# One reordering and one reshaped load in a load-bound decode kernel: denominators and last transposition moved, part of w2 in eight-row transfers

## Chip, cores, metric

One core of one Trainium2 chip. The metric is device time in microseconds (us) of one execution. The kernel before has a median of 191.76 us over six runs (190.99 to 192.43). The profiled run of the kernel before took 190.90 us, less than any of the six. A number read from a profile is therefore compared with profiled runs, a median with medians.

## The reference, cut to what matters

```python
xn = layernorm(x)                         # x: 2 x 1 x 448
q  = xn @ wq                              # 16 heads of 256
k, v = the last 4096 rows of the caches   # 8 kv heads, 2 batches: 16 pairs of 2 MB each
p  = softmax(q @ k.T / 16)
A  = (p @ v) @ wo
h  = xn @ w1 + b1
B  = (h * tanh(softplus(h))) @ w2         # w1: 448 x 1792, w2: 1792 x 448
return x + A + B
```

It is 77.7 MB of caches and weights read once, against little arithmetic. The kernel must keep the loads going.

## The kernel before: the parts concerned

`P` is 128. `i` counts the 16 pairs (kv head, batch). All large loads are issued by SP (SyncE), in program order. PE is TensorE, ACT ScalarE, DVE in the profiles VectorE. `kt` is the transposed k, `den` the sum in a softmax denominator, `psA` the accumulated output. A load counts as landed at the last count of its completion semaphore, the counter that others wait on.

```python
x_bf ... nc.scalar.dma_start(...)         # x, then b1, issued by ACT
for lo, hi in ((0, SC), (SC, NS)):        # wq in two parts, by SP
    nc.sync.dma_start(out=w, in_=wq_in[:, lo:hi, :])
# ... cut ...
def load_dense():
    dense["w1"] = v_tile(NS * HF)...
    nc.sync.dma_start(out=dense["w1"], in_=B_w1...)
    dense["w2"] = v_tile(NX * NF * D).rearrange("p (x c d) -> p x c d", x=NX, c=NF)
    nc.sync.dma_start(                    # one transfer, 128 rows
        out=dense["w2"], in_=B_w2.rearrange("(x q c) d -> q x c d", x=NX, q=P))
# ... cut ...
def turn_p(s):                            # VectorE: transpose exp(scores); then, for the second half:
    nc.vector.transpose(out=pT[:], in_=p_t.pop(s)[:])
    # ... cut ...  sums from the row sums (two VectorE instructions)
    nc.tensor.matmul(den[:], lhsT=ones_f[:], rhs=sums[:], start=True, stop=True)
    nc.vector.reciprocal(out=state["rec", i][:], in_=den[:])
# ... cut ...
load_k(0)
load_dense()
load_k(1)
project(); build_q(0); build_q(1); turn(0)
NFIX = 5                                  # so many last pairs use 64 narrow matmuls (values_fixed)
for i in range(NK + KA):                  # NK = 16, KA = 2
    if i + 2 < NK:
        load_k(i + 2)
    if i < NK:
        load_v(i, ...); # load_wo every second pair
        for half in range(NH):
            s = i * NH + half
            if s + 1 < NSTEP: turn(s + 1) # VectorE: transpose half of k
            scores(s)                     # PE, then ACT exp
            if s >= 1: turn_p(s - 1)
            if half == 0 and i > KA: close(i - KA - 1)   # finish a head, mix in wo
    if i == NK:
        turn_p(NSTEP - 1)
        close(i - KA - 1)
    # ... cut: dense_in at i == 0, dense_out at i == 1 ...
    if i >= KA: values(i - KA) or values_fixed(i - KA)
    if i >= NK: close(i - KA)
```

In this document k1 is the second k to be loaded (`load_k(1)`), head 13 is pair 13, and so on; "small" transfers are the eight new ones.

The softmax here doesn't subtract the row's maximum and nothing guards it: scores larger than these inputs give would overflow.

Of the kernel before, what the change touches and what calls it, by code (L numbers as in the profile page):

```python
# [12 lines left out]
FP32 = mybir.dt.float32  # L13
# [21 lines left out]
def kernel(  # L35
# [13 lines left out]
    nc = tc.nc  # L49
    P = 128  # L50
    Q = 32
    NQ = P // Q

    Bsz, Sq, D = A_x.shape
    _, Hkv, Sk, Dh = A_k_cache.shape
    HqDh = A_wq.shape[1]
    Hq = HqDh // Dh
    rep = Hq // Hkv
# [6 lines left out]
    NX = 2  # L65
    NS = D * NX // P
    HW = HqDh // NX
    HF = F // NX
    HH = Hq // NX
    NF = HF // P  # L70
    ND = Dh // P
    NB = Dh // (2 * Q)
    NE = 2
# [15 lines left out]
    small = ctx.enter_context(tc.tile_pool(name="small", bufs=3))  # L89
# [9 lines left out]
    b1_sb = consts.tile([1, F], BF16)  # L99
# [3 lines left out]
    def v_tile(n):  # L103
        t = v_pool.tile([P, T * Dh], BF16, tag="v", name="v")
        return t[:, 0:n]
# [6 lines left out]
    for lo, hi in ((0, SC), (SC, NS)):  # L112
# [18 lines left out]
        out=rstd[:], in_=mv[:, 1:2], func=ACT.Sqrt, bias=eps_t[:], scale=1.0  # L131
# [80 lines left out]
    def add(lhsT, w, start=False, stop=False):  # L212
        for n in range(NO):
            nc.tensor.matmul(  # L214
                part(n),
                lhsT=lhsT,
                rhs=w[:, n * DO : (n + 1) * DO],
                start=start,
                stop=stop,
                tile_position=(0, n * Q),  # L220
                skip_group_check=True,
            )
# [47 lines left out]
    act_bf = consts.tile([P, NF, NX, Bsz], BF16)  # L270
    dense = {}

    def load_dense():
        dense["w1"] = v_tile(NS * HF).rearrange("p (s n) -> p s n", s=NS)
        nc.sync.dma_start(  # L275
            out=dense["w1"],
            in_=B_w1.rearrange("r (x n) -> (r x) n", x=NX).rearrange("(p s) n -> p s n", s=NS),
        )
        dense["w2"] = v_tile(NX * NF * D).rearrange("p (x c d) -> p x c d", x=NX, c=NF)
        nc.sync.dma_start(  # L280
            out=dense["w2"], in_=B_w2.rearrange("(x q c) d -> q x c d", x=NX, q=P)
        )

    def dense_in():
        w1_v = dense.pop("w1").rearrange("p s (q c) -> p s c q", c=NF)
        b1_v = b1_sb[:].rearrange("o (x q c) -> o x c q", x=NX, c=NF)
        hT_ps = ps_m.tile([P, NF, NX, Bsz], FP32, tag="m", name="hT_ps")
        for c in range(NF):
            for s in range(NS):
                nc.tensor.matmul(  # L290
                    hT_ps[:, c, :, :].rearrange("p x b -> p (x b)"),
                    lhsT=w1_v[:, s, c, :],
                    rhs=xs[:, s, :, :].rearrange("p x b -> p (x b)"),
                    start=(s == 0),
                    stop=False,
                    skip_group_check=True,
                )
            for x in range(NX):
                nc.tensor.matmul(
                    hT_ps[:, c, x, :],  # L300
                    lhsT=b1_v[:, x, c, :],
                    rhs=ones[:, :],
                    start=False,
                    stop=True,
                    skip_group_check=True,
                )
        shape = [P, NF, NX, Bsz]
        h_sb = consts.tile(shape, FP32, name="h_sb")
        nc.vector.tensor_copy(out=h_sb[:], in_=hT_ps[:])
        u_sb = consts.tile(shape, FP32, name="u_sb")  # L310
        nc.scalar.activation(out=u_sb[:], in_=h_sb[:], func=ACT.Exp)
        t_sb = consts.tile(shape, FP32, name="t_sb")
        nc.vector.scalar_tensor_tensor(
            out=t_sb[:], in0=u_sb[:], scalar=2.0, in1=u_sb[:], op0=ALU.add, op1=ALU.mult
        )
        den = consts.tile(shape, FP32, name="den_sb")
        nc.vector.tensor_scalar(
            out=den[:], in0=t_sb[:], scalar1=2.0, scalar2=None, op0=ALU.add
        )
        nc.vector.reciprocal(out=den[:], in_=den[:])  # L320
        nc.vector.tensor_tensor(out=t_sb[:], in0=t_sb[:], in1=den[:], op=ALU.mult)
        nc.vector.tensor_tensor(out=act_bf[:], in0=h_sb[:], in1=t_sb[:], op=ALU.mult)

    def dense_out():
        w2_sb = dense.pop("w2")
        for x in range(NX):
            for c in range(NF):
                add(act_bf[:, c, x, :], w2_sb[:, x, c, :])


    NSTEP = len(heads) * NH
# [63 lines left out]
    def turn_p(s):  # L395
        pT = p_pool.tile([P, TH * Q], BF16, tag="pT", name="pT", bufs=7)
        nc.vector.transpose(out=pT[:], in_=p_t.pop(s)[:])  # L397
        pT_t[s] = pT
        i, half = divmod(s, NH)
        if half != NH - 1:  # L400
            return
        rs = state.pop(("rs", i))
        sums = small.tile([P, rep], FP32, tag="sums", name="sums")
        nc.vector.tensor_scalar(  # L404
            out=sums[:], in0=hsel, scalar1=rs[:, 0:1], scalar2=None, op0=ALU.mult
        )
        nc.vector.scalar_tensor_tensor(  # L407
            out=sums[:], in0=hsel, scalar=rs[:, 1:2], in1=sums[:], op0=ALU.mult, op1=ALU.add
        )
        den = ps_m.tile([P, rep], FP32, tag="m", name="den")  # L410
        nc.tensor.matmul(den[:], lhsT=ones_f[:], rhs=sums[:], start=True, stop=True)  # L411
        state["rec", i] = small.tile([P, rep], FP32, tag="rec", name="rec", bufs=4)
        nc.vector.reciprocal(out=state["rec", i][:], in_=den[:])  # L413

    NP = 2
    NR = NP * rep
# [1 line left out]
    def values(i):  # L418

        po = ps_o.tile([NR, NP * Dh], FP32, tag="o", name="o")  # L420
        v = v_t.pop(i)
        for u in range(T // NP):
            half, uh = divmod(u, TH // NP)
            nc.tensor.matmul(  # L424
                po[:],
                lhsT=pT_t[i * NH + half][:, uh * NP * Q : (uh + 1) * NP * Q : HS],
                rhs=v[:, u * NP : (u + 1) * NP, :].rearrange("p t d -> p (t d)"),
                start=(u == 0),
                stop=(u == T // NP - 1),
            )  # L430
        o_sb = small.tile([NR, NP * Dh], FP32, tag="o_sb", name="o_sb", bufs=1)
        nc.scalar.copy(out=o_sb[:], in_=po[:])  # L432
        state["o", i] = o_sb

    def scale_o(i, o):
        kvh, b = heads[i]
        if b == 0:
            state["oT"] = small.tile([P, ND, rep, Bsz], BF16, tag="oT", name="oT")
        nc.vector.tensor_tensor(  # L439
            out=state["oT"][:, :, :, b],  # L440
            in0=o,
            in1=state.pop(("rec", i))[:].unsqueeze(1).to_broadcast([P, ND, rep]),
            op=ALU.mult,
        )

# [14 lines left out]

    def values_fixed(i):

        pq = ps_q.tile([P, NP * ND * NR], FP32, tag="q", name="q")
        po = pq[:, 0 : ND * rep].rearrange("p (c h) -> p c h", c=ND)
        vv = v_t.pop(i).rearrange("p t (m c) -> p t c m", c=ND)
        for t in range(T):
            half, th = divmod(t, TH)
            pTv = pT_t[i * NH + half][:].rearrange("p (t c) -> p t c", t=TH)
            for c in range(ND):
                nc.tensor.matmul(  # L470
                    po[:, c, :],
                    lhsT=vv[:, t, c, :],
                    rhs=pTv[:, th, 0:Q:HS],
                    start=(t == 0 and c == 0),
                    stop=(t == T - 1),
                    skip_group_check=True,
                )
        scale_o(i, po)
# [19 lines left out]
    build_q(0)  # L498
    build_q(1)
    turn(0)  # L500
    NFIX = 5

    def close(i):
        if i < NK - NFIX:
# [5 lines left out]
    for i in range(NK + KA):  # L510
# [3 lines that stand above are left out]
            load_v(i, (0, T) if i < NK - 1 else (0, T // 2, 3 * T // 4, T))  # L514
            kvh, b = heads[i]
            if b == Bsz - 1:
                load_wo(kvh, parts=1 if i < NK - 1 else 2)
            for half in range(NH):
                s = i * NH + half
                if s + 1 < NSTEP:  # L520
                    turn(s + 1)
                scores(s)
                if s >= 1:
                    turn_p(s - 1)
                if half == 0 and i > KA:
                    close(i - KA - 1)
            if i + 2 < NK:
                build_q(i + 2)
        if i == NK:
            turn_p(NSTEP - 1)  # L530
            close(i - KA - 1)
        if i == 0:
            dense_in()
        if i == 1:
            dense_out()
        if i >= KA:
            if i - KA < NK - NFIX:
                values(i - KA)
            else:
                values_fixed(i - KA)  # L540
        if i >= NK:
            close(i - KA)
# [37 lines left out]
```

## Time and profile before

| | before |
|---|---|
| time, median of 6 | 191.76 us |
| span of the profiled run (190.90 us) | 189.1 us |
| bytes read | 77.67 MB |
| DMA queue of SP, share of 16 engines' span | 97.1% |
| PE busy | 77% |
| VectorE waits for k | 37.2 us |
| last load (second half of the last wo) lands | 183.55 to 185.33 us, by engine |

### The profile page before, as it was taken

The numbers are of one execution on the slowest core, as the hardware profiler recorded it, in microseconds if no ns is written. First come the engines' busy times: TensorE is split into PE (matmuls) and PEld (weight loads), VectorE is DVE, ScalarE is ACT, GpSimd is POOL, SyncE is SP. The second block draws the span as 40 slices with busy tenths as digits, with TensorE's granted clock in tenths as the row PEclk, the third lists the DMA queues.
The fourth block names the chain that finished last, engine by engine and source line by source line (L and its number), as shares of the span: only waits on it lengthen the run. The fifth ranks groups of instructions, "written<-read, shape, count | busy, mean of one in ns | idle before, by whom it ended". The sixth has DMA issues, their size and how long they took to land.

```text
span 189.1 us, 3026 instructions
## 1 busy us (share of the span) xinstructions
PE 145.6 (77%) x1202; PEld 71.1 (38%) x1202; DVE 113.5 (60%) x193; ACT 32.0 (17%) x81; POOL 27.6 (15%) x139
## 2 busy tenths in 40 slices
PE   0142992696997799949996899779994996598973
PEld 0142381142442435323533235233532344252572
DVE  5705506988839392857658582939376764839221
ACT  6000110112122013111212022201221121110201
POOL 8004430031130030203030023003020300000000
PEclk9999996699999789997999699978999799955855
DMA  6999999999999999999999999999999999999990
GB/s 215 419 444 414 431 438 426 437 428 430 418 423 433 437 421 431 426 437 407 448 430 428 433 419 433 430 426 418 442 437 426 414 435 433 425 430 423 415 381 27
DMA packets 7816, 77.86 MB, mean 412 GB/s; under 512 B 757, under 2 KB 2809, under 8 KB 3322
## 3 DMA queue, kind: packets, MB, share of 16 engines
q1 hardware_dynamic: 7796, 77.66, 97.1%
q8 instruction: 9, 0.15, 0.3%
q14 instruction: 5, 0.04, 0.1%
q10 hardware_dynamic: 6, 0.01, 0.0%
HBM read 77.67 MB, written 0.00 MB: 411 GB/s over the span
## 4 chain that ended last, share of the span: by engine, by line
DMA 70%; DVE 21%; PE 6%; SPq 1%; issue 1%; ACT 0%; ACTq 0%
DMA k<-in_A_k_cache_dram 70%; DVE kt L364 14%; DVE pT L397 4%; PE q L470 3%; PE sc L376 1%; PE den L411 1%; DVE sums L407 1%; PE psA L214 1%; DVE sums L404 0%; SPq L114 0%; DVE oT L439 0%; SPq L275 0%; SPq L280 0%; SPq L338 0%; DVE rec L413 0%
## 5 line engine op out<-in xcount | busy, mean ns | idle before, releaser
L364 DVE STREAM_TRANSPOSE kt<-k 128x2048 f32<-128x2048 f32 x32 | 73.3, 2292 | 37.2 <-DMA k<-in_A_k_cache_dram 37.2
L376 PE MATMUL sc<-kt,qdiag 128*128 128x512 bf16 x256 | 75.2, 445 | 9.9 <-DVE kt L364 9.7
L376 PEld LDWEIGHTS <-qdiag 128*128 128x128 bf16 x256 | 25.6, 109 | 48.9 <-issue 28.0
L264 POOL COPY qdiag<-qrep 32x8 bf16<-32x8 bf16 x128 | 23.3, 215 | 122.9 <-PE sc L376 108.3
L424 PE MATMUL o<-v,pT 128*4 128x512 bf16 x176 | 39.8, 379 | 0.0
L386 ACT ACTIVATE p<-sc 128x512 bf16<-128x512 f32 x32 | 19.1, 597 | 105.1 <-PE sc L376 103.1
L424 PEld LDWEIGHTS <-pT 128*4 128x4 bf16 x176 | 14.4, 87 | 25.7 <-issue 5.8
L397 DVE STREAM_TRANSPOSE pT<-p 128x512 bf16<-128x512 bf16 x32 | 21.5, 672 | 0.0
L411 PE MATMUL den<-sums,ones_f 128*128 128x2 f32 x32 | 5.9, 253 | 15.5 <-DVE sums L407 15.4
L411 PEld LDWEIGHTS den<-sums,ones_f 128*128 128x128 f32 x32 | 5.6, 203 | 21.8 <-DVE sums L407 18.2
L432 ACT COPY o_sb<-o 4x512 f32<-4x512 f32 x11 | 6.3, 576 | 32.3 <-PE o L424 32.3
L413 DVE RECIPROCAL rec<-den 128x2 f32<-128x2 f32 x16 | 2.7, 171 | 12.6 <-PE den L411 12.6
L470 PEld LDWEIGHTS <-v 128*128 128x128 bf16 x320 | 9.1, 101 | 1.6 <-issue 1.1
L470 PE MATMUL q<-pT,v 128*128 128x2 bf16 x320 | 9.2, 165 | 0.3 <-DVE oT L439 0.3
L235 PE MATMUL qT_ps<-xs,v 128*128 128x4 bf16 x112 | 3.3, 166 | 6.2 <-DMA v<-in_A_wq_dram 3.4
L452 PE MATMUL q<-ident_f,o_sb 4*128 4x4 f32 x44 | 7.0, 261 | 0.0
L214 PE MATMUL psA<-wo,oT 128*2 128x112 bf16 x128 | 3.8, 256 | 3.5 <-DVE oT L439 3.5
L386 ACT ACTIVATION_READ_ACCUMULATOR p<-sc 128x1 f32 x32 | 6.2, 195 | 0.0
L452 PEld LDWEIGHTS q<-ident_f,o_sb 4*128 4x128 f32 x44 | 6.0, 206 | 0.2
L235 PEld LDWEIGHTS <-v 128*128 128x128 bf16 x112 | 3.1, 104 | 6.4 <-DMA v<-in_A_wq_dram 6.4
L439 DVE TENSOR_TENSOR oT<-q,rec 128x4 bf16<-128x4 f32 x5 | 0.8, 150 | 7.3 <-PE q L470 7.3
L454 DVE COPY osum<-q 128x4 f32<-128x4 f32 x11 | 1.8, 162 | 4.3 <-PE q L452 4.3
(52 smaller groups left out, 42.6 us busy)
## 6 DMA issues: line engine op xcount, KB each, us to landing
k<-in_A_k_cache_dram SPq DMA_DIRECT2D x16, 2048.0 KB, 31.4
v<-in_A_v_cache_dram SPq DMA_DIRECT2D x15, 2048.0 KB, 34.7
v<-in_B_w_dram SPq DMA_DIRECT2D x2, 1568.0 KB, 21.0
wo<-in_A_wo_dram SPq DMA_DIRECT2D x7, 448.0 KB, 31.5
v<-in_A_wq_dram SPq DMA_DIRECT2D x1, 2048.0 KB
v<-in_A_wq_dram SPq DMA_DIRECT2D x1, 1536.0 KB, 10.9
v<-in_A_v_cache_dram SPq DMA_DIRECT2D x1, 1024.0 KB, 28.6
v<-in_A_v_cache_dram SPq DMA_DIRECT2D x2, 512.0 KB, 27.3
```

The lines of the kernel that those rows point to most:

```text
L214: nc.tensor.matmul(part(n), lhsT=lhsT, rhs=w[:, n * DO : (n + 1) * DO], start=start, stop=stop, tile_position=(0, n * Q), skip_group_check ...
L235: nc.tensor.matmul(qT_ps[:, hh, e, :], lhsT=wq_v[s][:, hh, e, :], rhs=xs[:, s, :, :].rearrange("p x b -> p (x b)"), start=(s == 0), stop=( ...
L264: nc.gpsimd.tensor_copy(out=tv[rows, :, e, j * Q : (j + 1) * Q : HS], in_=qrep[rows, :, h0 : h0 + rep, e, x, b],)
L364: nc.vector.transpose(out=kt[:].bitcast(FP32), in_=k[:, half * TH * Dh : (half + 1) * TH * Dh].bitcast(FP32),)
L376: nc.tensor.matmul(psc[:], lhsT=qdiag[i % NW][:, n * NE + e, :], rhs=ktv[:, n, e, :, :], start=(n == 0 and e == 0), stop=(n == NB - 1 and ...
L386: nc.scalar.activation(out=p_sb[:], in_=psc[:].rearrange("p t c -> p (t c)"), func=ACT.Exp, scale=scale, accum_out=state["rs", i][:, s % N ...
L397: nc.vector.transpose(out=pT[:], in_=p_t.pop(s)[:])
L411: nc.tensor.matmul(den[:], lhsT=ones_f[:], rhs=sums[:], start=True, stop=True)
L424: nc.tensor.matmul(po[:], lhsT=pT_t[i * NH + half][:, uh * NP * Q : (uh + 1) * NP * Q : HS], rhs=v[:, u * NP : (u + 1) * NP, :].rearrange( ...
L432: nc.scalar.copy(out=o_sb[:], in_=po[:])
L452: nc.tensor.transpose(pqv[:, u, c, :], ov[:, u, c, :], ident_f[0:NR, 0:NR])
L470: nc.tensor.matmul(po[:, c, :], lhsT=vv[:, t, c, :], rhs=pTv[:, th, 0:Q:HS], start=(t == 0 and c == 0), stop=(t == T - 1), skip_group_chec ...
```

## The change

Three things, and one that goes with the first: four instead of five last heads use the 64 narrow matmuls (`NFIX`). The matmul that adds up a head's softmax denominator moves from just behind the sums to just ahead of the head's values, so that PE need not wait for VectorE. The last transposition of p moves ahead of the closing of head 13. And one seventh of w2 (the last 128 of 896 hidden columns of each half) moves from 128 partitions to 64, in eight transfers of eight rows four partitions apart. Each of the eight transfers is spread over eight DMA engines, so eight engines carry bytes that all sixteen shared before.

```diff
+    PE2 = P // 2
+    NA = HF // P - 1
+    NF = NA + (HF - P * NA) // PE2
 ...
-        nc.sync.dma_start(
-            out=dense["w2"], in_=B_w2.rearrange("(x q c) d -> q x c d", x=NX, q=P)
-        )
+        nc.sync.dma_start(
+            out=t[:, :, 0:NA, :], in_=w2_in[:, 0 : P * NA, :].rearrange("x (q c) d -> q x c d", q=P)
+        )
+        rest = w2_in[:, P * NA : HF, :].rearrange("x (q c) d -> q x c d", q=PE2)
+        for q0 in range(0, PE2, Q):
+            for j in range(4):
+                rows = slice(q0 + j, q0 + Q, 4)
+                nc.sync.dma_start(out=t[rows, :, NA:NF, :], in_=rest[rows, :, :, :])
 ...  (dense_in and dense_out use 64 rows for the last two chunks; a memset clears hT_ps)
+    def denominator(i):
         den = ps_m.tile([P, rep], FP32, tag="m", name="den")
-        nc.tensor.matmul(den[:], lhsT=ones_f[:], rhs=sums[:], start=True, stop=True)
+        nc.tensor.matmul(
+            den[:], lhsT=ones_f[:], rhs=state.pop(("sums", i))[:], start=True, stop=True
+        )
 ...
+        state["rec", i] = denominator(i)      # first in values(i) and values_fixed(i)
 ...
-    NFIX = 5
+    NFIX = 4
 ...
+                if s == NSTEP - 1:
+                    turn_p(s)
 ...
         if i == NK:
-            turn_p(NSTEP - 1)
             close(i - KA - 1)
```

More of the change, by code (lines that the diff above doesn't have):

```diff
@@ L69 @@
     HH = Hq // NX
-    NF = HF // P
+    PE2 = P // 2
+    NA = HF // P - 1
+    NF = NA + (HF - P * NA) // PE2
     ND = Dh // P
@@ L271, with hidden @@
     dense = {}
+    def hidden(c):
+        if c < NA:
+            return slice(0, P), slice(c, P * NA, NA)
+        return slice(0, PE2), slice(P * NA + c - NA, HF, NF - NA)
     def load_dense():
@@ L278, in load_dense @@
         )
-        dense["w2"] = v_tile(NX * NF * D).rearrange("p (x c d) -> p x c d", x=NX, c=NF)
+        t = v_tile(NX * NF * D).rearrange("p (x c d) -> p x c d", x=NX, c=NF)
+        w2_in = B_w2.rearrange("(x f) d -> x f d", x=NX)
         nc.sync.dma_start(
-            out=dense["w2"], in_=B_w2.rearrange("(x q c) d -> q x c d", x=NX, q=P)
+            out=t[:, :, 0:NA, :], in_=w2_in[:, 0 : P * NA, :].rearrange("x (q c) d -> q x c d", q=P)
         )
+        rest = w2_in[:, P * NA : HF, :].rearrange("x (q c) d -> q x c d", q=PE2)
[3 more added lines that the diff above has]
+                nc.sync.dma_start(out=t[rows, :, NA:NF, :], in_=rest[rows, :, :, :])
+        dense["w2"] = t
     def dense_in():
-        w1_v = dense.pop("w1").rearrange("p s (q c) -> p s c q", c=NF)
-        b1_v = b1_sb[:].rearrange("o (x q c) -> o x c q", x=NX, c=NF)
+        w1 = dense.pop("w1")
         hT_ps = ps_m.tile([P, NF, NX, Bsz], FP32, tag="m", name="hT_ps")
+        nc.vector.memset(hT_ps[:], 0.0)
         for c in range(NF):
+            rows, cols = hidden(c)
             for s in range(NS):
                 nc.tensor.matmul(
-                    hT_ps[:, c, :, :].rearrange("p x b -> p (x b)"),
-                    lhsT=w1_v[:, s, c, :],
+                    hT_ps[rows, c, :, :].rearrange("p x b -> p (x b)"),
+                    lhsT=w1[:, s, cols],
                     rhs=xs[:, s, :, :].rearrange("p x b -> p (x b)"),
@@ L299, in dense_in @@
                 nc.tensor.matmul(
-                    hT_ps[:, c, x, :],
-                    lhsT=b1_v[:, x, c, :],
+                    hT_ps[rows, c, x, :],
+                    lhsT=b1_sb[:, x * HF + cols.start : x * HF + cols.stop : cols.step],
                     rhs=ones[:, :],
@@ L327, in dense_out @@
             for c in range(NF):
-                add(act_bf[:, c, x, :], w2_sb[:, x, c, :])
+                rows, _ = hidden(c)
+                add(act_bf[rows, c, x, :], w2_sb[rows, x, c, :])
     NSTEP = len(heads) * NH
@@ L402, in turn_p @@
         rs = state.pop(("rs", i))
-        sums = small.tile([P, rep], FP32, tag="sums", name="sums")
+        sums = small.tile([P, rep], FP32, tag="sums", name="sums", bufs=4)
         nc.vector.tensor_scalar(
@@ L409, in turn_p @@
         )
+        state["sums", i] = sums
+    def denominator(i):
         den = ps_m.tile([P, rep], FP32, tag="m", name="den")
-        nc.tensor.matmul(den[:], lhsT=ones_f[:], rhs=sums[:], start=True, stop=True)
-        state["rec", i] = small.tile([P, rep], FP32, tag="rec", name="rec", bufs=4)
-        nc.vector.reciprocal(out=state["rec", i][:], in_=den[:])
+        nc.tensor.matmul(
+            den[:], lhsT=ones_f[:], rhs=state.pop(("sums", i))[:], start=True, stop=True
+        )
+        rec = small.tile([P, rep], FP32, tag="rec", name="rec")
+        nc.vector.reciprocal(out=rec[:], in_=den[:])
+        return rec
     NP = 2
@@ L436, in scale_o @@
         kvh, b = heads[i]
+        rec = state.pop(("rec", i))
         if b == 0:
@@ L441, in scale_o @@
             in0=o,
-            in1=state.pop(("rec", i))[:].unsqueeze(1).to_broadcast([P, ND, rep]),
+            in1=rec[:].unsqueeze(1).to_broadcast([P, ND, rep]),
             op=ALU.mult,
@@ L461, in values_fixed @@
     def values_fixed(i):
+        state["rec", i] = denominator(i)
         pq = ps_q.tile([P, NP * ND * NR], FP32, tag="q", name="q")
```

## The prediction

> **What bounds the kernel now.** I read the page first, the slices before the table of engines.
>
> ```profile
> span 189.1 us, 3026 instructions
> ...
> DMA  6999999999999999999999999999999999999990
> GB/s 215 419 444 414 431 438 426 437 428 430 418 423 433 437 421 431 426 437 407 448 430 428 433 419 433 430 426 418 442 437 426 414 435 433 425 430 423 415 381 27
> ...
> q1 hardware_dynamic: 7796, 77.66, 97.1%
> ...
> DMA 70%; DVE 21%; PE 6%; SPq 1%; issue 1%; ACT 0%; ACTq 0%
> ```
>
> No slice between the first and the last has a DMA share under 9, and PE, the busiest engine, has 77%. So the sixteen DMA engines carry a stream that never breaks, and the kernel ends when it has passed, plus a tail. To see how strictly this holds I took the packet records of the trace and joined packets whose end meets another's start; they fall into sixteen sequences, one for each DMA engine, each with the same 47 transfers. From 6 us on no sequence has a hole: a 2 MB transfer takes 4.86 us on every engine (431 GB/s), from k1's completion (28.18 us on the first engine) to that of the last part of wo (183.23), 155.05 us. What differs between engines is a lag against the first. Eight of the sixteen each get one 16 KB instruction fetch between 17.4 and 178.2 us, and each costs its engine 1.42 us for good; four 8 KB fetches cost others 0.5 to 0.85. The two engines with x's rows and the one with b1 are not among the eight. At the end the eight lag 1.51 to 1.81 us, six others 0 to 0.87 and the last two 1.05 and 1.69. The last part of wo thus lands between 183.55 and 185.33. That imbalance is plainly what the w2 part of the change is after.
>
> Then the waits of the queue that issues the loads, in the timeline of SP:
>
> ```profile
> 3.27 0.98 SPq L338 DMA_DIRECT2D k<-in_A_k_cache_dram  x2
> 8.46 0.33 SPq L348 DMA_DIRECT2D v<-in_A_v_cache_dram  x1
> 8.84 0.43 SPq L338 DMA_DIRECT2D k<-in_A_k_cache_dram  x1
> 15.15 0.33 SPq L348 DMA_DIRECT2D v<-in_A_v_cache_dram  x1
> 16.98 0.38 SPq L357 DMA_DIRECT2D wo<-in_A_wo_dram  x1
> 21.63 0.33 SPq L338 DMA_DIRECT2D k<-in_A_k_cache_dram  x1
> 25.39 0.33 SPq L348 DMA_DIRECT2D v<-in_A_v_cache_dram  x1
> ```
>
> These times are landings of transfers which these loads have nothing to do with: the first part of wq landed at 8.45, k0 at 16.96, w1 at 21.57, w2 at 25.33. The program has eight completion semaphores for loads, given out in turn in program order, and a load waits until the last user of its semaphore has landed in full. So at most eight transfers are under way, whatever their size. With 2 MB ones that is some 30 us of work in the queue, and the waits cost nothing.
>
> Last the tail, in the chain of waits:
>
> ```profile
> 177.61 1.65 PE q L470 x64
> 179.26 0.02 issue
> 179.28 0.17 DVE oT L439
> 179.45 0.62 DVE pT L397
> 180.06 0.12 DVE sums L404
> ...
> 180.21 0.23 DVE sums L407
> ...
> 180.49 0.58 PE den L411 x2
> 181.07 0.47 PE psA L214 x16
> 181.55 1.81 PE q L470 x64
> ...
> 183.60 1.86 PE q L470 x64
> ...
> 185.70 0.65 PE psA L214 x16
> ```
>
> From 179.26 to 181.07 PE does no product of its own: oT must come before the last pT on VectorE, and the denominator after its sums.
>
> [...] x (two rows) has two data packets on two engines, b1 one on one. Eight rows thus give eight engines[...]. [...] 1.03 us from the first issue (0.74) to its first packet, 0.75 for the output; I use these.
>
> **The change part by part.**
>
> *Denominators.* PE now does den just before the values of the same head, when the sums are long there. That removes PE's waits at L411, 15.4 us in nine places, but off the path: DMA sets the pace. The reciprocals wait behind PE in VectorE's order instead; VectorE idles 37.2 us for k, so it is hidden. One head fewer is summed the 64-matmul way. Worth 0 before the tail.
>
> *Tail.* The last pT and sums come ahead of oT of head 13. From the end of scores(30), 174.49, I lay out: scores(31) 2.5 at once (saves the 0.58 of den) to 177.0; den 0.5 and values(13) 1.7 to 179.2; oT 0.25; mix 0.5 to 180.0; den 0.58; values(14) 1.85 to 182.4; den 0.58; values(15) 1.86 to 184.85, but its last quarter lands at 184.21 and needs 0.5 after that, so no later bound; oT 0.25; mix 0.65 to 185.75. PE's clock in the tail is unsure by a few tenths, so 185.75 to 185.95 against 186.35: 0.4 to 0.6 saved, and close to the landing of wo's last part (185.33 plus eight of sixteen matmuls, 0.3).
>
> *w2, bytes.* Its 16 packets of 6,272 B per engine (235 ns apart) become 16 of 5,376. The gaps for 1,792, 6,272, 12,544 and 16,384 B (70.5, 235, 465, 607 ns) give 0.0367 ns per byte, so 202 ns: 0.53 us less on all sixteen. The lower eight get 16 packets of 1,792 B, 1.13, and eight semaphore writes of 6 ns: 1.18 more. Relative shift 1.18 us[...]. By itself it could bring the last landing forward by 0.3 to 0.5, or put it back [...].
>
> *w2, number of transfers.* This decides it. Eight small transfers use up the eight semaphores. In the built order of the changed kernel small 1 and 2 go at once, small 3 waits for wq's first part, 4 for b1, 5 for wq's second part, 6 for k0, 7 for w1, and small 8 for the big part of w2, which is just ahead of it in the queue. k1, which was issued at 3.27 us, stands behind small 8. When the big part of w2 has landed nothing of size is queued: a hole.
> - Big part lands: 25.33 − 0.53 = 24.80 (its slowest engine had the fetch at 17.38, before anything changed).
> - small 8 issued 24.86, k1 0.39 later: 25.25.
> - The kernel's own start is the model of a restart: issue 0.74, first engine through its eight rows at 7.24, so 6.50. With the output's latency 0.28 less. k1 done on the first engine: 31.5 to 31.75, against 28.18: +3.3 to +3.6.
> - Old lags are wiped out, and with them the balancing; new ones are drawn. At the kernel's start the eight fetching engines lagged up to 0.45; plus 1.42 that is 1.87, as before 1.81.
> - Nothing can catch up, since after k1 the same bytes pass at the same rate: the whole stream is 3.3 us later, give or take 0.5. While it waits the engines only move 0.23 MB.
> After small 8 the next semaphores belong to small transfers that have landed, so eight large ones queue up at once and no second hole follows.
>
> *Sum:* stream +3.3, tail −0.5: +2.8 us, 191.76 + 2.8 = 194.5 (+1.5%).
>
> **Rivals.**
> 1. *No hole; balance works.* Last landing 184.9, tail −0.6: 191.1. It asks that k1 be issued early. Against it: every semaphore wait of SP above holds to the landing within 0.1 us, and the built order has these waits.
> 2. *Smaller hole.* [...] against: packets after an 8 KB fetch took 0.8 us and after a 16 KB fetch 1.1 us instead of 0.61, so a broken stream restarts slowly.
> 3. *Bigger loss.* A second hole, if loads behind k1 also wait late, or PE (busy nine tenths in many slices) can't follow after the hole: 196 to 197. For it: VectorE now waits for PE in each head; against: PE loses 15 us of waits.
> 4. *Tail gives nothing,* because DMA or PE's halved clock sets it: 195.0.
>
> **Range and chances.** The hole's parts are uncertain by some 0.7 us together, the tail by 0.4, and the times before spread over 0.7. 8 in 10: 193.0 to 196.0. Slower by over 2% begins at 195.6, 1.1 above the middle: 0.15. Faster by over 2% is below 187.9, under what the bytes take: 0.01. Within 2%: 0.84.
>
> **What will show it.** SP's timeline should have the third small transfer at 8.5 us, the seventh at 21.6, the eighth near 24.9 and k1 near 25.3; the DMA share should drop in the slice or two at 24 to 27 us, and VectorE's first wait for k1 should grow by 3 us. kt of the last k should start near 171.8 instead of 168.46. den's waits at PE should be gone, and PE should have no gap of a microsecond after values(13). I am wrong if k1 is issued before 20 us, if the DMA share stays at 9 there, or if the stream's end moves by under 1.5 us.

"The lower eight" are the eight engines of the small transfers. That there are eight is in the trace of after; which eight is not, and that the engines with a 16 KB fetch are not among them was the assumption. The halved clock of rival 4 is the 0.50 granted to PE from 180 us on in the profile of before.

## The result, and the profile after

| | before | after |
|---|---|---|
| time, median of 6 | 191.76 us (190.99 to 192.43) | 194.75 us (194.62 to 195.06) |
| time of the profiled run | 190.90 us | 194.78 us |
| span of the profiled run | 189.1 us | 193.0 us |
| ratio after / before | | 1.0157, 95% interval 1.0133 to 1.0182 |

Ratios here and below are the mean time of one kernel's runs over that of the other's of the same rounds, so not quite the ratio of the medians quoted. The change costs 1.6%: clearly slower, and within the 2% that counts as the same. 194.5 with 193.0 to 196.0 had been predicted.

The page of the kernel after; the slices are 4.8 us wide:

```profile
span 193.0 us, 2991 instructions
...
DMA  6999859999999999999999999999999999999990
GB/s 218 424 446 403 367 140 428 435 428 428 413 442 431 428 428 427 431 431 424 428 428 423 431 423 430 435 435 413 442 431 431 428 424 433 431 431 418 416 395 37
...
q1 hardware_dynamic: 7988, 77.67, 95.7%
...
DMA 80%; DVE 13%; PE 3%; SPq 1%; issue 1%; ACT 0%; ACTq 0%
```

The hole is in the fifth and sixth slices (19.3 to 29.0 us), 367 and 140 GB/s. The other slices are as before: what is lost there is never made up. The chain of waits of the kernel after (start, length, what; its longest pieces) walks straight through the hole:

```profile
2.69 22.10 DMA v<-in_B_w_dram
24.81 0.67 SPq L296
25.52 7.71 DMA k<-in_A_k_cache_dram
33.25 2.31 DVE kt L381
...
163.07 25.63 DMA v<-in_A_v_cache_dram
188.75 0.60 PE q L496 x16
189.59 0.71 PE psA L216 x16
```

The big part of w2, issued at 2.69, lands at 24.79. Only then can SP issue the last small transfer, and behind it k1, which lands at 33.23 (30.18 before). At the end the chain is a v load, up to 188.70, with two short stages of PE behind it. SP's queue of the kernel after, and the durations of the small issues (min/median/max in ns):

```profile
3.18 22.30 SPq L296 DMA_DIRECT2D v<-in_B_w_dram  x8
25.52 0.91 SPq L355 DMA_DIRECT2D k<-in_A_k_cache_dram  x2
26.48 0.43 SPq L365 DMA_DIRECT2D v<-in_A_v_cache_dram  x1
```

```profile
L296 SPq DMA_DIRECT2D v<-in_B_w_dram x8: 665/670/867, 3.2 to 24.8; - x8
```

The eight issues start at 3.18, 4.10, 8.13, 8.84, 11.75, 16.62, 21.63 and 24.81 us: small 3 at the landing of wq's first part, 5 at that of its second part, 6 at k0's, 7 at w1's, 8 at that of the big part of w2. VectorE's waits for k (us in total, times, longest), of the kernel before and of the kernel after:

```profile
DVE kt L364 <- DMA k<-in_A_k_cache_dram: 37.2, 14, 8.7
```

```profile
DVE kt L381 <- DMA k<-in_A_k_cache_dram: 50.1, 13, 12.1
```

The longest (k1) went from 8.7 to 12.1. The sum, 12.9 us more than before, is not the hole's: it is 37.0 in w2_only, which has the hole, and 55.0 in reorder_only, which has none (both kernels follow below). With the new order VectorE no longer waits for PE's denominators (12.6 us before, 1.0 after), and waits longer for k instead.

**A measure of the hole.** Two sums over the trace's packet records will serve for every run. *Idle*: between 6 and 175 us, how far the number of packets of more than 4 bytes under way (loads and instruction fetches) falls short of sixteen, over time, divided by 16. *Slow*: between 22 and 40 us, by how much packets took longer than the median for their size, divided by 16. Before: 0.08 and 0.03 us. After: 3.12 and 0.98. After the hole, k1's first packets took up to 1.89 us instead of 0.61. Together the kernel after has 4.0 us more than the one before, and the first engine is through k1 at 32.31 us instead of 28.18, 4.1 later. By 187.45 (183.23 before) it is through the last load, 4.2 later, so nothing came back on the way.

### The profile page after: what moved, and what is told of

Read it like the earlier page. It is cut to its first block, busy times and chain, and to the rows that moved or that the text cites. A ratio compares the mean times of both kernels' runs of the same rounds, so it can differ in the third digit from the quotient of the medians.

```text
span 193.0 us, 2991 instructions
## 1 busy us (share of the span) xinstructions
PE 140.3 (73%) x1175; PEld 70.1 (36%) x1175; DVE 113.7 (59%) x196; ACT 32.5 (17%) x82; POOL 27.1 (14%) x139
## 4 chain that ended last, share of the span: by engine, by line
DMA 80%; DVE 13%; PE 3%; SPq 1%; issue 1%; ACT 0%; ACTq 0%
DMA k<-in_A_k_cache_dram 56%; DMA v<-in_A_v_cache_dram 13%; DMA v<-in_B_w_dram 11%; DVE kt L381 9%; DVE pT L414 2%; PE hT_ps L306 2%; PE hT_ps L315 1%; SPq L116 0%; PE psA L216 0%; SPq L296 0%; PE q L496 0%; SPq L283 0%; SPq L355 0%; DVE sums L421 0%; DVE den_sb L336 0%
## 5 line engine op out<-in xcount | busy, mean ns | idle before, releaser
L393 PE MATMUL sc<-kt,qdiag 128*128 128x512 bf16 x256 | 68.7, 415 | 17.0 <-DVE kt L381 16.2
L393 PEld LDWEIGHTS <-qdiag 128*128 128x128 bf16 x256 | 23.9, 102 | 54.2 <-issue 26.3
L448 PE MATMUL o<-v,pT 128*4 128x512 bf16 x192 | 43.4, 379 | 0.0
L448 PEld LDWEIGHTS <-pT 128*4 128x4 bf16 x192 | 15.8, 87 | 21.8
L456 ACT COPY o_sb<-o 4x512 f32<-4x512 f32 x12 | 6.9, 575 | 36.6 <-PE o L448 36.6
L306 PE MATMUL hT_ps<-xs,v 128*128 128x4 bf16 (+1 forms) x56 | 4.0, 190 | 12.5 <-DVE hT_ps L302 12.5
L496 PE MATMUL q<-pT,v 128*128 128x2 bf16 x256 | 7.6, 165 | 1.4 <-DMA v<-in_A_v_cache_dram 1.4
L306 PEld LDWEIGHTS <-v 128*128 128x128 bf16 (+1 forms) x56 | 3.3, 144 | 13.0 <-issue 12.9
L496 PEld LDWEIGHTS <-v 128*128 128x128 bf16 x256 | 7.3, 99 | 1.8 <-DMA v<-in_A_v_cache_dram 1.8
L237 PEld LDWEIGHTS <-v 128*128 128x128 bf16 x112 | 3.1, 104 | 4.8 <-DMA v<-in_B_w_dram 3.0
L431 PE MATMUL den<-sums,ones_f 128*128 128x2 f32 x32 | 4.8, 220 | 0.0
```

The costliest lines, as they stand in the source:

```text
L237: nc.tensor.matmul(qT_ps[:, hh, e, :], lhsT=wq_v[s][:, hh, e, :], rhs=xs[:, s, :, :].rearrange("p x b -> p (x b)"), start=(s == 0), stop=( ...
L306: nc.tensor.matmul(hT_ps[rows, c, :, :].rearrange("p x b -> p (x b)"), lhsT=w1[:, s, cols], rhs=xs[:, s, :, :].rearrange("p x b -> p (x b) ...
L393: nc.tensor.matmul(psc[:], lhsT=qdiag[i % NW][:, n * NE + e, :], rhs=ktv[:, n, e, :, :], start=(n == 0 and e == 0), stop=(n == NB - 1 and ...
L431: nc.tensor.matmul(den[:], lhsT=ones_f[:], rhs=state.pop(("sums", i))[:], start=True, stop=True)
L448: nc.tensor.matmul(po[:], lhsT=pT_t[i * NH + half][:, uh * NP * Q : (uh + 1) * NP * Q : HS], rhs=v[:, u * NP : (u + 1) * NP, :].rearrange( ...
L456: nc.scalar.copy(out=o_sb[:], in_=po[:])
```

## The experiments

Theory: the loss is a hole in the stream, made by the order in which transfers take eight completion semaphores; the reordering is a small gain. Rivals: the reordering costs; eight-engine transfers cost; each small transfer costs; the late k1 costs by idling VectorE and PE. Eleven kernels ran, four to six times each, all correct. Idle and slow are of the profiled run. A kernel's "before" is the kernel before run on the same chip in the same rounds (medians 191.4 to 191.8).

| kernel | median us | ratio to before | idle us | slow us |
|---|---|---|---|---|
| after | 194.75 | 1.0157 | 3.12 | 0.98 |
| reorder_only | 190.61 | 0.9951 | 0.08 | 0.00 |
| w2_only | 194.97 | 1.0188 | 3.23 | 1.00 |
| four_four | 191.44 | 0.9989 | 0.25 | 0.27 |
| one_transfer | 191.90 | 1.0019 | 0.08 | 0.85 |
| six_two | 192.16 | 1.0041 | 0.56 | 1.03 |
| seven_one | 193.98 | 1.0127 | 2.57 | 0.86 |
| eight_on_sixteen | 195.00 | 1.0175 | 3.03 | 0.96 |
| k1_ahead | 194.86 | 1.0169 | 3.49 | 0.72 |
| spread_eight | 190.94 | 0.9970 | 0.09 | 0.00 |
| spread_sixteen | 191.65 | 1.0005 | 0.08 | 0.80 |
| two_full | 190.76 | 0.9965 | 0.07 | 0.00 |

### Each part of the change alone

**reorder_only**: the kernel after with the w2 loading, dense_in and dense_out of before.

```diff
-        nc.sync.dma_start(out=t[:, :, 0:NA, :], ...)      # and the eight small transfers
+        nc.sync.dma_start(out=dense["w2"], in_=B_w2.rearrange("(x q c) d -> q x c d", x=NX, q=P))
```

> The kernel before with the denominators and the last transposition reordered, w2 loaded as before. My theory (the order is hidden behind the loads except in the tail, where it saves 0.4 to 0.6 us): ratio to before 0.996 to 0.999, about 191.3 us, k1 issued near 3.7 us and the DMA share unbroken. Rival (VectorE, which now waits for PE's denominators in its order, or one head fewer summed with 64 matmuls, costs time in the steady part): over 193 us, part of the loss is here.

190.61 us, ratio 0.9951 (0.9929 to 0.9973). The reordering is a gain, 1.1 us between the medians and so twice what I had thought. But the profiled runs, from which the estimate was made, took 190.90 and 190.51: 0.4 us, as estimated. Kernels with the old order vary more (before, in these rounds, 190.83 to 192.04; w2_only 194.49 to 196.16) than this one (190.39 to 190.87); that the old tail makes the longer runs is likely and not shown. What each of the parts (denominators, last transposition, NFIX) gives was not run. The rival falls. The end of this kernel's chain of waits:

```profile
168.39 17.08 DMA wo<-in_A_wo_dram
185.47 0.04 issue
185.51 0.46 PE psA L214 x8
```

PE is now ready before the last load and does only the last eight matmuls behind it, where before it ran from 181 to 186.35 without a load to wait for.

**w2_only**: the kernel before with the w2 part of the diff and nothing else.

```diff
     (w2 part of the change as above)
-    NFIX = 4; denominator(i); turn_p(NSTEP - 1) early
+    NFIX = 5; denominators and last transposition as before
```

> The kernel before with only the w2 part changed. My theory (the hole at 24 to 27 us is the whole loss): the full hole, first engine through k1 at 32.3 us as in the changed kernel against 28.2 before, ratio 1.017 to 1.022, 195.0 to 196.0 us, so 0.4 to 0.6 us slower than the changed kernel. Rival (the loss needs both parts): under 193 us.

194.97 us, ratio 1.0188 (1.0156 to 1.0219, so whether it is slower by 2% is unclear), just under the stated 195.0; the first engine is through k1 at 32.41. The hole is all there without the reordering. The reordering on top of it is worth little: 0.2 us between the medians (194.97 to 194.75), nothing between the profiled runs (194.68 and 194.78), and the intervals of the two ratios overlap. The windows view of the two kernels without the reordering, from the last k's landing for 9 us (stretch, its length, busy time and instructions of PE, PEld, DVE, ACT and POOL, then PE's granted clock, the DMA share and GB/s), shows where they differ. The kernel before:

```profile
168.40:177.50 9.10, 8.29 (x85) 4.21 (x84) 6.87 (x9) 1.38 (x4) 0.00 (x0) 0.56 1.01 426
```

w2_only:

```profile
172.30:181.50 9.20, 6.99 (x79) 3.49 (x76) 6.87 (x9) 1.14 (x5) 0.00 (x0) 0.81 1.01 425
```

PE had a clock of 0.56 before and 0.81 here, with nearly the same work (one profile each). In w2_only PE gets to the last v before it has landed even with the old order (it waits 0.41 us for it), so the loads set the end and the order has little left to save. Why the clock was granted so differently is not settled; I made no run on it.

### Where k1 stands among the small transfers

Three kernels move only the issue of k1. Its position decides on which semaphore it waits.

**four_four**, **six_two**, **seven_one**: k1 after the fourth, sixth or seventh small transfer.

```diff
-        for q0 in range(0, PE2, Q): ...          # all eight
+        rest_rows(0, CUT)                        # CUT = 4, 6 or 7
+        load_k(1)
+        rest_rows(CUT, 8)
 ...
     load_dense()
-    load_k(1)
```

> The changed kernel, the same eight small transfers on eight engines, but k1 issued after the fourth, which lets it go at 12.1 us when the second part of wq has landed. My theory (the order of taking semaphores makes the hole, not the small transfers): no hole, DMA share 9 in every slice, 191.0 to 191.8 us, 3 us under the changed kernel. The balance alone is then left: by my lags the lower eight engines end later by 0.65 us, so the last landing is 0.3 to 0.5 us later than with one transfer of 64 rows. Rival A (eight small transfers or eight-engine transfers cost their time by themselves): 194 us and over. Rival B (the author's aim, balance pays): 0.3 to 0.6 us under the kernel with one transfer.

191.44 us, as expected, 3.3 us under the kernel after, with the same transfers, bytes and engines. SP's queue of four_four:

```profile
3.28 6.30 SPq L298 DMA_DIRECT2D v<-in_B_w_dram  x4
11.85 0.35 SPq L361 DMA_DIRECT2D k<-in_A_k_cache_dram  x1
16.71 9.46 SPq L298 DMA_DIRECT2D v<-in_B_w_dram  x4
26.21 0.43 SPq L361 DMA_DIRECT2D k<-in_A_k_cache_dram  x1
```

k1 goes out at the landing of wq's second part, eleven microseconds before the engines run out of work (22.7). Rival A (the small transfers cost their time by themselves) falls. It is faster than one_transfer, not slower, as I had expected; see below. A trace of a hole stays: idle 0.25, slow 0.27. k2 is issued at 26.21 and its engines are free at about 27.9, so 1.7 us ahead was not quite enough.

> The changed kernel, k1 issued after the sixth of the eight small transfers. By the order of the semaphores k1 then waits for the landing of w1, 21.6 us, a microsecond before the big part of w2 has passed on the first engine. My theory (only a wait on the big part of w2 itself makes the hole): k1 issued at 21.6 to 22.0, no slice with a DMA share under 9, time within 0.5 us of the kernel with four ahead (191.44): 191.1 to 191.9. Rival (each small transfer ahead of k1 costs its share): six eighths of the loss of 3 to 4 us over the kernel with four ahead, so 193.5 and over.

192.16 us, above the 191.1 to 191.9 that I had stated. k1 was issued at 21.72, as foreseen, but the first engines had finished the big part of w2 at 22.7, and a microsecond ahead is too late. Of k1's first sixteen packets eight took 0.83 to 1.52 us instead of 0.61, and at k2 the stream thinned again. The page of six_two:

```profile
DMA  6999999999999999999999999999999999999980
GB/s 227 419 439 413 405 398 355 425 436 425 422 428 429 429 424 430 432 432 416 442 429 430 429 424 423 432 436 425 436 418 436 416 442 424 429 432 422 417 357 18
```

The DMA share shows nothing, for packets under way count as busy even if they crawl; the GB/s row shows it (405, 398, 355). Idle and slow make 1.5 us over reorder_only, and the median is 1.55 over it; but the profiled run was a long one (192.85), 2.3 over reorder_only's. In it the first engine is through the last load 1.7 us later than in reorder_only and the last engine 2.6 later, so the engines had also drifted apart, for a reason that I have not looked for. The rival (a cost for each transfer ahead of k1) would have had 193.5.

> The changed kernel, k1 issued after the seventh small transfer, so that it waits for the big part of w2. My theory: nearly the full hole. k1 is issued near 24.85 instead of 25.52 (one issue of 0.67 us less), so 0.6 to 0.8 us under the changed kernel: 193.9 to 194.3 us. One transfer more ahead of k1 than in the kernel with six costs 2.5 us or more. Rival (a cost for each small transfer): 0.4 us over the kernel with six.

193.98 us (four runs of 193.97 to 194.21). One 28 KB transfer more ahead of k1 costs 1.8 us, because k1 now waits for the big part of w2. I had said 2.5 or more over six_two; the time itself is as stated, six_two was the one mis-estimated. The page and SP's queue of seven_one:

```profile
DMA  6999869999999999999999999999999999999991
```

```profile
24.86 0.35 SPq L361 DMA_DIRECT2D k<-in_A_k_cache_dram  x1
```

So 4, 6, 7 and 8 small transfers ahead of k1 give 191.44, 192.16, 193.98 and 194.75: not a line, but what the time of k1's issue (11.85, 21.72, 24.86, 25.52) against the end of the queue (22.7) would make of it. No run changed the number of semaphores; that it is eight is in the program and in the traces of before and after (the loads count up semaphores 100 to 103 and 107 to 110, in turn), and the positions of k1 fit it.

### Eight engines, or eight transfers

**eight_on_sixteen**: reorder_only, with w2's last seventh on all 128 partitions, loaded by eight transfers of sixteen rows, for sixteen engines (an estimate from the completion counts of 4 bytes: 8 for eight rows, 16 for 128).

```diff
+        nc.sync.dma_start(out=dense["w2"][:, :, 0 : NF - 1, :], in_=w2_in[:, :, 0 : NF - 1, :])
+        for q0 in range(0, P, 16):
+            rows = slice(q0, q0 + 16)
+            nc.sync.dma_start(
+                out=dense["w2"][rows, :, NF - 1, :], in_=w2_in[rows, :, NF - 1, :])
```

> The kernel with only the order changed (190.61), its last eighth of the columns of w2 on 128 partitions as before, but loaded by eight transfers of sixteen rows, which sixteen engines share. My theory (the number of transfers, not the eight engines, makes the hole): k1 issued near 25.5, DMA share 8 and 5 in two slices, 194.2 to 195.2 us. Rival (eight engines loaded twice hold up the other eight): no loss, under 191.5.

195.00 us, and the same hole. The page of eight_on_sixteen:

```profile
GB/s 218 424 442 420 350 154 428 431 431 428 417 442 424 431 424 432 431 428 435 421 431 424 430 420 429 431 435 414 441 435 428 431 424 430 435 428 424 411 390 33
```

So it is the number of transfers, whatever engines they use. (The seventh of w2 is called an eighth in this expectation and in that of spread_sixteen; the edits take a seventh.) The rival (eight engines loaded twice hold up the others) falls. The issue of these small transfers on sixteen engines took less than half of the 670 ns of those on eight:

```profile
L284 SPq DMA_DIRECT2D v<-in_B_w_dram x8: 311/312/518, 3.2 to 25.2; - x8
```

### A late k1, or a hole

**k1_ahead**: the kernel after with k1 issued ahead of w2.

```diff
+        load_k(1)
         t = v_tile(NX * NF * D)...
 ...
     load_dense()
-    load_k(1)
```

> The changed kernel with k1 ahead of w2 in the queue, all eight small transfers behind w2 as before. k1 lands early, near 27 us, but the small transfers now wait in turn up to k1 and the big part of w2, and k2 behind them. My theory (a hole in the stream anywhere costs its length): the hole moves to 27 to 31 us, time as the changed kernel, 194.2 to 195.3. Rival (the loss is the late k1, for which VectorE and PE stand idle early on): most of the loss gone, 192 us or less.

194.86 us: no gain. The page of k1_ahead, and SP's queue:

```profile
DMA  6999984999999999999999999999999999999991
```

```profile
3.78 26.70 SPq L297 DMA_DIRECT2D v<-in_B_w_dram  x8
30.53 0.44 SPq L356 DMA_DIRECT2D k<-in_A_k_cache_dram  x1
```

The hole has moved by one slice and k2 stands behind it. k1 landed early (VectorE begins its transposition at 26.64 us, at 33.25 in the kernel after), and VectorE's longest wait for a k fell from 12.1 to 5.4 us, which was worth nothing: k2 and all loads behind it are late instead. The rival falls.

### Does moving bytes between engines pay, once there is no hole?

**one_transfer**: the 64 rows in one transfer, which sixteen engines share (by the same estimate).

```diff
+        nc.sync.dma_start(out=t[0:PE2, :, NA:NF, :], in_=rest)
```

> The changed kernel, the 64-partition part of w2 loaded by one transfer of 64 rows, which sixteen engines share. My theory: no hole and no shift of bytes between engines, so the same as the kernel with only the order changed, 191.1 to 191.5 us; k1 issued near 3.7 us. Rival (the layout on 64 partitions with its extra matmuls and the memset costs something): 193 us and over.

191.90 us, where 191.1 to 191.5 was expected, and 1.3 us above reorder_only although there is no idle. The slow sum is 0.85. The small packets took 89.6 ns in the mean and up to 161, against 74.0 in seven_one and spread_eight, which load the same 64 partitions eight rows at a time; but they make only 0.13 of the sum. 0.67 of it is in the 16 KB packets of k1, which ran beside them and took up to 1.1 us instead of 0.61. Why these packets were slow is not shown.

**spread_eight** and **spread_sixteen**: the eight small transfers of the kernel after (of eight_on_sixteen), two ahead of k1, three ahead of k2, three ahead of v0.

```diff
     load_dense()
+    rest_rows(0, 2)
     load_k(1)
+    rest_rows(2, 5)
 ...
             load_k(i + 2)
+        if i == 0:
+            rest_rows(5, 8)
```

> The changed kernel, the eight small transfers spread so that large loads always stand queued: two ahead of k1, three ahead of k2, three ahead of v0. No hole and, unlike four ahead of k1, 4 us of room at every wait (k1 issued at 8.5 to 9.5, k2 near 22, v0 near 29). What is left of the change is its order and its balance, so against spread_sixteen this shows the balance alone. My theory (the shift of 1.2 us between the halves is too large: a lower engine that already fetched instructions twice now ends last): last landing 0.3 to 0.6 us later than spread_sixteen, 191.0 to 191.5 us. Rival (balance pays): 0.3 us or more under spread_sixteen, near 190.2.

> The control: the kernel with only the order changed, w2's last eighth in eight transfers of sixteen rows on all sixteen engines, spread over the queue in the same way. My theory: no hole, as fast as the kernel with only the order changed (190.61): 190.5 to 191.0 us. Rival (eight more transfers cost some tenths each through their issue on the queue of SP): over 192.

spread_eight: 190.94 us, idle and slow as in reorder_only; it has every transfer of the change and none of its loss. spread_sixteen: 191.65 (five runs; a sixth of 194.73 was slow and is left out), not 190.5 to 191.0. It has no idle either but 0.80 of slow packets (0.73 of it in large packets beside the small ones), and its stream ends 1.0 us later on its first engine than reorder_only's. With these slow packets, whose cause is not shown, it was no clean control, and the comparison that I had planned (the rival "balance pays" won it by 0.7 us) says nothing of the balance.

**two_full**: reorder_only with w2 in two transfers of 128 rows.

```diff
+        for lo, hi in ((0, NF - 1), (NF - 1, NF)):
+            nc.sync.dma_start(out=dense["w2"][:, :, lo:hi, :], in_=w2_in[:, :, lo:hi, :])
```

> The kernel with only the order changed, w2 loaded by two transfers of 128 rows (six sevenths and one seventh of its columns). One transfer more, as with the 64 rows in one transfer (191.90 us), but on all 128 partitions. My theory (that kernel lost its 1.3 us to the order-only kernel, 190.61, because sixteen engines wrote to 64 partitions, where the mean small packet took 90 ns instead of 74): no such packets over 74 to 80 ns, 190.5 to 191.0 us. Rival (one more transfer or another split of w2 costs it): 191.6 us and over.

190.76 us, no slow packets. So it was the row pattern of one_transfer, 64 rows at once (90 ns for a small packet in the mean), not the additional transfer, that cost; what it is in that pattern, no run here shows.

The fair pair for the balance is spread_eight against reorder_only: 190.94 against 190.61, ratios to before 0.9970 (0.9940 to 1.0001) and 0.9951 (0.9929 to 0.9973). In their profiles the last load lands on the first engine at 183.00 against 183.42, and on the last at 185.85 against 185.47: early engines are earlier and the late one later. A gain is not seen; a loss of a few tenths is likely and not settled, for the intervals overlap and there is one profile of each.

### Do the sums add up?

Idle plus slow over reorder_only, against the time over reorder_only, both of the profiled runs (reorder_only 190.51): after 4.0 and 4.3; w2_only 4.2 and 4.2; seven_one 3.4 and 3.5; six_two 1.5 and 2.3; k1_ahead 4.1 and 4.2; eight_on_sixteen 3.9 and 4.3; one_transfer 0.9 and 1.4; spread_sixteen 0.8 and 1.0; four_four 0.4 and 1.0; spread_eight 0.0 and 0.3; two_full 0.0 and 0.3. What is left is 0 to 0.5 us, with and without eight-engine transfers alike, save 0.8 in six_two, as said there. No kernel beats reorder_only, which is 0.5% faster than before and 2.1% faster than after by the medians.

## Why the prediction was right

*The hole.* Right in mechanism and in its clock times. Stated and measured: small 3 at 8.5 and 8.13; small 7 at 21.6 and 21.63; the big part of w2 landing at 24.80 and 24.79; small 8 near 24.86 and at 24.81; k1 at 25.25 and 25.52. The semaphores were read off the built order and SP's landings of before, and four_four, six_two and seven_one move the hole by them alone. k1_ahead moves it without changing its cost; eight_on_sixteen makes it without eight engines.

*Its size.* Too small. Stated: k1 done on the first engine at 31.5 to 31.75, stream +3.3 us; measured 32.31 and +4.1 to +4.2. The term that was off is the restart. Issuing a small transfer took SP 0.67 us, not the 0.39 of a large one (0.3), and from k1's issue to the first engine's completion it was 6.8 us, not the 6.2 to 6.5 taken from the kernel's start (0.3 or more).

*The order.* Hidden in the steady part: right. The tail term, 0.4 to 0.6, was right for the order alone (0.4 between the profiled runs, 1.1 between the medians), but not in the kernel after. There the stream's end is 4.5 us later than before (185.33 to 189.80) and the last mix ends 3.95 later (186.35 to 190.30), so the tail did give 0.5; but w2_only, with the old order, has the same (its last mix ends at 190.19). What gave it is that the loads, not PE, set the end behind the hole: the mechanism of rival 4, which expected 195.0. The sum +2.8 hit the measured +3.0 partly by luck: in the profiled runs, from which the estimate was made, the change costs 3.9 us (190.90 to 194.78), since the stream was 0.8 to 1.2 later than stated (4.1 on its first engine, 4.5 at its last landing, against 3.3); the median of before lies 0.9 above its profiled run and made this good.

*The balance.* "Wiped out" by the restart: right. After the hole the engines stood within 0.62 us of each other at k1, where w2's slowest engine had been 1.6 behind. The statement that, by itself, it could go either way was right to be cautious; it shows no gain.

*Signs.* DMA share down in slices five and six; PE's waits at the denominator gone; no idle of a microsecond on PE between values(13) and the end of the values (0.64 at most); VectorE's wait for k1 longer by 3.4 us (3 stated). kt of the last k was to start near 171.8, and started at 172.79, for the same reason as the size above. One thing I had not foreseen: the new memset of hT_ps stands in VectorE's order behind k1's transposition, so PE waited 12.5 us for it at the start of dense_in. It lay within the hole's shadow and cost nothing that I can find; spread_eight has the same memset (PE waits 7.3 us for it) and is within 0.3 us of reorder_only.

*Rivals.* The smaller hole would have needed a quick restart; 0.98 us of slow packets show the contrary. The second hole (196 to 197) did not come: every slice from the seventh up to the tail is at 9. Rival 4 is told above.

*Two readings that do not hold.* 187.9 us is not under what the bytes take: by their sum they take 180. And after the four 8 KB fetches a packet took 0.83, 0.85, 1.14 and 1.15 us, not 0.8 each. Neither carries the result.

## What to carry to other kernels

In these kernels eight completion semaphores, taken in turn, limited how many transfers were under way, not how many bytes: eight transfers of 28 KB in a row drained the stream (idle 3.12 us against 0.08), and k1 behind them was issued only at 25.52 us, after the big part of w2 had landed at 24.79. The same eight spread among large ones (spread_eight) left idle at 0.09. In a queue that does the same, spread small transfers among large ones, and see that each large load is issued before the queue runs dry; here 1.0 us ahead (six_two) cost 1.5 us of idle and slow packets, 1.7 us (four_four) half of one, 3.0 us (spread_eight, at v0) none. Where loads set the pace, look first at whether a change leaves them an unbroken queue, before counting what it saves in bytes per engine.

## What else the traces showed

- The restart of a stream: 0.75 us from issue to the first packet for the output (before), and 1.08 for k1 after the hole (after: 25.52 to 26.60), whose first packets then took 1.07 to 1.89 us instead of 0.61. A hole of 3.0 us of idle cost 4.1.
- The issue of small transfers: eight rows on eight engines took SP 0.67 us each (after), as many bytes in sixteen rows 0.31 (eight_on_sixteen). That the number of engines is the reason is not shown: one_transfer's 64 rows took 0.72.
- Instruction fetches: each 16 KB fetch took 1.42 us from one DMA engine's share of a load stream that has no slack, on eight engines (the rebuilt packet sequences of before), which at the end lagged 1.5 to 1.8 us behind the first.
